# Built forms in a third place, their second part stored first, one raw piece loaded later, and several splits moved

## The chip, the cores and the metric

The kernel runs on one core of a Trainium2 chip. The metric is the device time of one execution in microseconds (us). The times of before are those of three runs; one more execution was profiled, and all rows of the trace come from that one.

## The reference

One input x of 2048 rows and 640 columns is normalized along its rows, without scale or shift. The output is the sum of x and two branches that both read the normalized rows, all in float32:

```python
x = A_x
xn = _layernorm(x, axis=-1)
a = jnp.einsum("bsd,ed->bse", xn, dft_hid_re)
b = jnp.einsum("bsd,ed->bse", xn, dft_hid_im)
y = jnp.einsum("ts,bse->bte", dft_seq_re, a) - jnp.einsum("ts,bse->bte", dft_seq_im, b)
h = jax.nn.gelu(jnp.einsum("bsd,df->bsf", xn, w1) + b1, approximate=True)
return x + y + (jnp.einsum("bsf,fd->bsd", h, w2) + b2)
```

The first branch is a Fourier transform along the hidden dimension (640) and along the sequence (2048), of which the real part is kept; its matrices are inputs. The second is a perceptron with 1536 hidden units.

## The kernel before

**Splits and products.** A float32 operand is split in two: a high part, made by ScalarE (ACT, `high`, line 190), and a low part, made by VectorE (DVE, `low`, line 193) from the operand and its high part. A product of two split operands is three matmuls (`product`, lines 304 to 306): high by high, high by low, low by high. `hidden` (line 326) does the same three by itself. Where the split is of a moving operand, PE can start on the high part and needs the low part one matmul later.

**Order.** The schedule is written out by hand: each engine runs its instructions in the order in which the Python text issues them, and waits only for what an instruction needs. Loads and stores that are issued with `nc.sync` stand in the queue of SP in the same order, those with `nc.gpsimd` in that of POOL.

**Places.** Most of the on-chip memory is a set of named places (`PLACES`, line 144): xab0 to xab3, xc01, xc23, as, r01, rt2. A place holds different things one after the other. When it is opened anew (`place`, `open_place`), the first write into it waits until the last reader of what was there is done. In the perceptron's last block the places hold the split weights: `W1[i]` (the columns of 128 hidden units) and `W2[i]` (their rows of w2). xc23 holds W2[3], W2[4] and W2[5].

**The perceptron.** It runs over four blocks of 512 rows, with twelve chunks of 128 hidden units each. The first block runs chunk by chunk; blocks 1 and 2 share their hidden products in pairs (`pair(k)`, k from 0 to 5, `LASTK` = 5); their hidden units are written to DRAM (`keep`), and `load_unit(i)` brings those of block 2 back as `units[i]` for the outputs of block 2. Around a pair, `beside_pair(k, at)` does work that has nothing to do with it: `prep_w` builds and stores pieces of the hidden transform's weights (`put_w`, line 443 stores them into `wits`), `turn_w` transposes the next raw ones, `put_z` brings the rows of block 3 together for transposing, and `split_unit` splits the hidden units that come next. `split_unit(2 * NF, units[0])` and `split_unit(2 * NF + 1, units[1])` serve the first two outputs of the next loop.

The next loop runs over p from 2 to 9 and does the outputs of block 2; from p = 8 on it also does the first two hidden products of block 3, whose rows have been transposed and split into `xt` by `between(p)`. `between(p)` also loads and splits again what w1 and w2 need (`prep_w1`, `load_w1`, `prep_w2`); w1's raw chunks have three buffers, so the load of one waits for the split of the one three before.

**The loop around the change** (line 1304) does block 3. It runs over i from 0 to 11. A step issues the hidden product of chunk i + 2 (15 matmuls), its gelu and split, the output of chunk i (15 matmuls), `between(2 + NU + i)` for i below 2 (that is p = 10 and 11), and `fourier_step(i)`. Steps 10 and 11 have no hidden product.

**Builds.** `fourier_step(i)` for i from 2 to 9 runs `build(k)` with k = i - 2. A build reads two raw chunks of 128 normalized rows from DRAM (`load_xr`, two steps ahead) and makes from them, by sums and splits, the weights of the transform along the sequence: a first part `xab` (128 partitions of 2 x 1280 numbers, 1280 KB) and a second part `xc` (2 x 896, 896 KB). In the order of the text a build makes most of `xab` first and `xc` last (`part(xc, ...)`, lines 666 and 667, whose ACT half is line 639). The first four builds (h = 1) are for the second half of the transform: their forms are stored to DRAM (`forms_ab`, `forms_c`, lines 1223 and 1224) and loaded again much later. The last four (h = 0) stay in place and are used at once. Builds 0 to 3 and builds 4 to 7 share the places xab0 to xab3. For the second part there are two halves of xc01 and two of xc23; before the change

- builds 0 and 2 use the first half of xc01 and builds 1 and 3 the second half,
- builds 4 and 5 use the two halves of xc01, builds 6 and 7 those of xc23,

so that builds 2, 3, 4 and 5 write where an earlier build was, and wait until that one's store has landed. Build 7's raw rows are loaded by POOL into the second half of xc23 itself, which is opened for that at i = 7 (`load_xr(7)`).

**Raw pieces.** The moving operand of the transform along the sequence comes from `cr` and `ci`, in pieces of four quadrants of 256 KB (`load_a`, line 509). `load_a(0)` and `load_a(1)` load the first two at i = 2. `turn` (line 530) transposes a piece in two halves, `form(n)` splits one half into a slot of `as`, and each entry of the Fourier stage that follows uses one form. `load_a(heir[g])`, issued after a piece's second half is turned, loads the next piece into the same buffer. The pool of raw pieces takes the memory of the raw w1 and w2 (`es_e.close()`), so it waits for their last splits.

**After the loop** ACT takes the five sums of block 3 out of PSUM (line 1383, `ob`), the rest of build 7 and the first entries follow, and from there PE runs through the stages "s" (along the sequence) and "y" (along the hidden dimension) to the end.

Of the kernel before, what the change touches and what calls it, by code (L numbers as in the profile page):

```python
# [15 lines left out]
P = 128  # L16
# [11 lines left out]
def kernel(  # L28
# [78 lines left out]
    NK = 4  # L107
# [385 lines left out]
    def load_a(g):  # L493

        for f in steps_of_load(g):
            f()
# [105 lines left out]
    def load_xr(k):  # L602
        if k >= len(builds):
            return
        h, c = builds[k]
        xr[k] = []
        if k in (0, len(builds) - 1):
            n = 2 if k else 0
            A["xcp", n] = place(f"xc{n}{n + 1}", (P, 2, 2, 7 * P))
        for half in range(2):  # L610
            if k == len(builds) - 1:

                r = A["xcp", 2][:, 1, half, :D].bitcast(F32)
            else:
                r = row_places[:, (2 * k + half) % NC]
            (nc.gpsimd if k == len(builds) - 1 else nc.sync).dma_start(r, xn[half * NS // 2 + h * NK + c])
            xr[k].append(r)

    def build(k, what="abc"):
# [3 lines left out]
            A["sums"] = out_pool.tile([P, 2, 9 * P], F32, tag="zo", bufs=1, name="sums")  # L623
        if k < NK:
            A["xab", c] = place(f"xab{c}", (P, 2, 10 * P))
        A["xc", c] = A["xcp", c // 2 * 2 if h == 0 else 0][:, c % 2]
        ab, xc = A["xab", c], A["xc", c]
        tmp = A["sums"][:, k % 2]

# [398 lines left out]
    def beside_pair(k, at):  # L1028
# [27 lines left out]
        if k == 1:  # L1056
            if at == 2:
                add_sum(0, 2, turn_sum(0, 2, rows, "yt", True))
            if at == 5:
                finish(0, 3, 4)  # L1060
                store_sums(0, 1, 2)
            if at == 3:
                A["wst"] = zo_tile("wst", (P, NB * DQ), F32R)
        if at == {1: 7, LASTK: 4}.get(k, 6):
            turn_w(0, j)
            turn_w(1, j)
# [18 lines left out]
        if k == LASTK - 1 and at in (7, 4):  # L1085
            for c in (12, 13) if at == 7 else (14, 15):
                ln_stats(c)
                scale_by_power(c)
        for n in steps.get(at, ()):
            prep_w(*((j - 1, 3 + n) if n < 0 else (j, n)))  # L1090
        if k == LASTK and at == 2:
# [2 lines left out]
        if k == LASTK and at == 8:  # L1094
            A["gs"] = place("xab1", (P, 5, TB), F32)
            for i in range(3, 8):
                load_unit(i)
            split_unit(2 * NF, units[0])
            for c in range(3 * NC, 4 * NC):
                ln_apply(c)  # L1100
        if k == LASTK and at == 7:
            A["s1"] = place("xab2", (P, ND, TB), F32)
        if k == LASTK and at == 4:
            Z["z"] = place("xab3", (P, NB, DQ), F32)
            put_z(Z["z"], A["rows_3"], nc.gpsimd, nc.sync)
            split_unit(2 * NF + 1, units[1])
            split_unit(2 * NF + 2, units[2])

    units = {}
# [67 lines left out]
    def between(p):  # L1177
# [20 lines left out]
        for n, q in {7: 1, 9: 2, 10: 3}.items():  # L1198
            if p == n:
                open_place(*PLACES[q])  # L1200
        for n in {2: (0,), 3: (1,), 7: (2,), 8: (3,), 9: (4, 5), 10: (6, 7, 8), 11: (9, 10, 11)}.get(p, ()):
            prep_w1(AGAIN[n], 2 * NF + n)
            load_w1(2 * NF + 3 + n)
        if p == 8:
# [1 line left out]
                load_w2(i, nc.gpsimd)  # L1206
        if p == 10:
            open_place(*PLACES[8])
        for n in {10: (9, 10), 11: (11,)}.get(p, ()):
            prep_w2(n)  # L1210
        if p == NU:
            A["s2"] = zo_tile("s2", (P, ND, TB))
            for k, key in ((0, "x"), (2, "us")):
# [3 lines left out]
    def fourier_step(i):  # L1217
        if 2 <= i < 2 + 2 * NK:
            k = i - 2
            build(k, "abc" if i < 9 else "a")  # L1220
            load_xr(k + 2)
            if k < NK:
                nc.sync.dma_start(forms_ab[k], A["xab", k].bitcast(F32))
                nc.sync.dma_start(forms_c[k], A["xc", k].bitcast(F32))
        if i == 9:
            A["r01"] = place("r01", (P, 2, 2, 2, TB), F32)
            turn(0, 0)
# [75 lines left out]
    load_xr(1)  # L1303
    for i in range(NF):
        g = 3 * NF + i
        if i == 2:
            es_e.close()
            A["raw"] = pool("rawp")
            load_a(0)
            load_a(1)  # L1310
        if i >= NF - 2:
            output(g)
        else:
# [1 line left out]
            gelu(g + 2, acc)  # L1315
            output(g)

        if i < 2:
            between(2 + NU + i)
        fourier_step(i)  # L1320


# [672 lines left out]
```

## Time and profile before

| what | value |
|---|---|
| median of 3 runs | 854.04 us |
| lowest and highest run | 853.31 and 854.73 us |
| the profiled execution | 855.07 us |
| its span, first to last instruction | 853.3 us |
| mean clock granted to PE | 0.999 of full speed |
| DMA moved | 171.72 MB, mean 201 GB/s |
| PE busy in 222 to 250 us | 28.00 of 28.00 us |
| ACT busy in 290.3 to 305.5 us | 8.15 of 15.20 us |

The span is what the trace covers; the profiled execution's own time is 1.8 us longer. PE is TensorE's matmuls, PEld its weight loads, DVE VectorE, ACT ScalarE, POOL GpSimd and SP SyncE. In a time line a row gives start and duration, engine, line, operation, the tiles written and read, and their count; in brackets stands how long the engine was idle before, and what released it. A row "A <- B: 3.1, 4, 1.4" of the waits says that A waited for B 3.1 us in total, 4 times, at most 1.4. Matmuls overlap: a matmul is listed with about 0.39 us, while the next one starts some 0.23 us after it.

### The profile page before, as it was taken

What the parts mean: (1) busy time and instruction counts of PE and PEld (TensorE: products, weight loads), DVE (VectorE), ACT (ScalarE), POOL (GpSimd) and SP (SyncE); (2) the same over time, 40 slices, a digit from 0 to 9 for tenths busy, and PEclk for the clock granted to TensorE, in tenths of its full rate; (3) what the DMA queues carried; (4) which work ended last, traced back from release to release, by engine and by line L of the source; (5) the groups of instructions that cost most, each with busy time, mean ns of one, the idle gap of its engine ahead of it and who ended that gap; (6) DMA issues with size and microseconds to landing.
All of it is one profiled execution on the core that took longest, in us unless ns stands there. A gap on an engine that the chain in (4) does not pass through costs nothing.

```text
span 853.3 us, 10719 instructions
## 1 busy us (share of the span) xinstructions
PE 842.1 (99%) x3719; PEld 694.8 (81%) x3719; DVE 695.1 (81%) x920; ACT 373.7 (44%) x546; POOL 90.5 (11%) x166
## 2 busy tenths in 40 slices
PE   9999999999999999999999999999999999999997
PEld 7888888888788867888888888888888888888886
DVE  6978888777666689799888878899688998867995
ACT  6655656645555554334443432323224332344350
POOL 3440023256200000000000000000000000010102
PEclk9999999999999999999999999999999999999999
DMA  7996569779879779586445795637357997175453
GB/s 233 289 263 167 122 172 299 236 236 365 263 217 347 310 141 205 133 186 150 141 112 156 246 280 140 157 101 217 133 166 231 251 245 283 50 276 180 117 149 87
DMA packets 194454, 171.72 MB, mean 201 GB/s; under 512 B 57920, under 2 KB 164928, under 8 KB 193888
## 3 DMA queue, kind: packets, MB, share of 16 engines
q1 hardware_dynamic: 181664, 134.53, 58.9%
q0 software_dynamic: 10560, 35.99, 12.0%
q10 hardware_dynamic: 2176, 0.52, 0.3%
q8 instruction: 29, 0.48, 0.2%
q14 instruction: 25, 0.20, 0.1%
HBM read 119.87 MB, written 47.19 MB: 196 GB/s over the span
## 4 chain that ended last, share of the span: by engine, by line
PE 82%; DMA 8%; DVE 4%; ACT 2%; issue 1%; SPq 1%; POOL 1%; DVEq 0%; POOLq 0%; ACTq 0%
PE banks L305 25%; PE banks L306 25%; PE banks L304 25%; PE banks L326 5%; DMA forms_c<-xc 3%; DMA w1r<-in_B_w_dram 1%; DMA w2r<-in_B_w_dram 1%; DMA raw<-in_A_dft_seq_re_dram 1%; DMA xab<-rt 1%; PE banks L695 1%; SPq L282 1%; DVE rt L530 1%; DMA wit<-wst 0%; ACT xc L639 0%; DVE as L193 0%
## 5 line engine op out<-in xcount | busy, mean ns | idle before, releaser
L190 ACT ACTIVATE as<-r 128x1024 fp32r<-128x1024 f32 x80 | 84.9, 1062 | 170.2 <-PE banks L306 146.5
L305 PE MATMUL banks<-as,xab 128*128 128x512 f32 (+1 forms) x375 | 146.0, 389 | 3.1 <-DVE as L193 3.1
L306 PE MATMUL banks<-as,xab 128*128 128x512 f32 (+1 forms) x375 | 145.5, 388 | 0.0
L304 PE MATMUL banks<-as,xab 128*128 128x512 f32 (+1 forms) x375 | 145.5, 388 | 0.0
L193 DVE TENSOR_TENSOR as<-r,as 128x1024 fp32r<-128x1024 f32 x80 | 97.2, 1216 | 37.9 <-ACT as L190 37.7
L304 PE MATMUL banks<-as,xc 128*128 128x512 f32 x244 | 94.9, 389 | 0.0
L305 PE MATMUL banks<-as,xc 128*128 128x512 f32 x244 | 94.9, 389 | 0.0
L306 PE MATMUL banks<-as,xc 128*128 128x512 f32 x244 | 94.9, 389 | 0.0
L305 PEld LDWEIGHTS banks<-as,xab 128*128 128x128 f32 x375 | 70.4, 188 | 19.1 <-DVE as L193 4.7
L304 PEld LDWEIGHTS banks<-as,xab 128*128 128x128 f32 x375 | 70.4, 188 | 14.6 <-ACT as L190 0.2
L306 PEld LDWEIGHTS banks<-as,xab 128*128 128x128 f32 x375 | 70.4, 188 | 14.4
L190 ACT ACTIVATE as<-rt 128x1024 fp32r<-128x1024 f32 x37 | 39.3, 1063 | 82.4 <-PE banks L306 62.7
L326 PE MATMUL banks<-xt,xab 128*128 128x512 f32 x240 | 57.4, 391 | 0.7 <-DVE xt L193 0.7
L193 DVE TENSOR_TENSOR as<-rt,as 128x1024 fp32r<-128x1024 f32 x37 | 45.0, 1216 | 11.8 <-ACT as L190 11.8
L326 PEld LDWEIGHTS banks<-xt,xab 128*128 128x128 f32 x240 | 44.7, 188 | 11.0 <-DVE xt L193 1.8
L305 PEld LDWEIGHTS banks<-as,xc 128*128 128x128 f32 x244 | 45.8, 188 | 9.5
L306 PEld LDWEIGHTS banks<-as,xc 128*128 128x128 f32 x244 | 45.8, 188 | 9.5
L304 PEld LDWEIGHTS banks<-as,xc 128*128 128x128 f32 x244 | 45.8, 188 | 9.5
L305 PE MATMUL banks<-hs,xc 128*128 128x512 f32 x120 | 46.8, 390 | 0.2 <-DVE hs L193 0.2
L306 PE MATMUL banks<-hs,xc 128*128 128x512 f32 x120 | 46.7, 389 | 0.0
L304 PE MATMUL banks<-hs,xc 128*128 128x512 f32 x120 | 46.7, 389 | 0.0
L1428 POOL DMA_DIRECT2D seed_x<-seeds x1 | 0.5, 546 | 401.4 <-DVE y L469 401.4
(307 smaller groups left out, 1719.9 us busy)
## 6 DMA issues: line engine op xcount, KB each, us to landing
raw<-in_A_dft_seq_re_dram SPq DMA_DIRECT2D x64, 256.0 KB, 5.3
raw<-in_A_dft_seq_im_dram SPq DMA_DIRECT2D x64, 256.0 KB, 5.2
w1r<-in_B_w_dram SPq DMA_DIRECT2D x144, 80.0 KB, 3.4
wit<-wst POOLq DMA_DIRECT2D x15, 384.0 KB, 4.3
wit<-wst POOLq DMA_DIRECT2D x20, 256.0 KB, 4.2
forms_ab<-xab SPq DMA_DIRECT2D x4, 1280.0 KB, 12.6
ws<-wit SPq DMA_DIRECT2D x13, 384.0 KB, 5.2
row<-xn SPq DMA_DIRECT2D x14, 320.0 KB, 8.3
```

The source lines that it names most:

```text
L190: nc.scalar.activation(h, s, AF.Copy)
L193: nc.vector.tensor_tensor(l, s, h.bitcast(F32), op=ALU.subtract)
L282: eng.dma_start(t[q * B : (q + 1) * B], v[q, :, :, f0 : f0 + P])
L304: nc.tensor.matmul(acc, wh, mh, start=first, stop=False, skip_group_check=goes_on)
L305: nc.tensor.matmul(acc, wh, ml, start=False, stop=False, skip_group_check=goes_on)
L306: nc.tensor.matmul(acc, wl, mh, start=False, stop=last, skip_group_check=goes_on)
L326: nc.tensor.matmul(acc, W1[i][:, a, j * P : (j + 1) * P], XT[j][:, b], start=n == 0, stop=n == len(steps) - 1)
L530: nc.vector.transpose(held(pieces[g][2], u).rearrange("p c (n i) -> p c n i", i=B), r.rearrange("p n (c i) -> p c n i", i=B))
L695: nc.tensor.matmul(wacc, warm[:, :P], warm, start=True, stop=True)
L1428: nc.gpsimd.dma_start(A["seed"], seeds[:, c0:c1])
```

## The change

1. **A third place.** The second part of build 3 goes to the second half of xc23, not to that of xc01. xc23 is opened in build 3 (i = 5), not with build 7's rows (i = 7). Builds 4 to 7 use the same places as before.
2. **Stores.** Of each of the first four builds, `forms_c` is stored before `forms_ab`.
3. **Raw pieces.** `load_a(0)` stays at i = 2, but behind the work that `between(12)` now does there; `load_a(1)` is issued at i = 7.
4. **Last splits of w1 and w2.** The six w1 splits that stood at p = 10 and 11, three each, stand at 10, 11 and 12, two each; of the three w2 splits there is one at each.
5. **First two units.** `split_unit` of unit 0 goes ahead of `prep_w` at place 8 of the last pair, and that of unit 1 ahead of `turn_w` at place 4.

```diff
@@ load_xr
-        if k in (0, len(builds) - 1):
-            n = 2 if k else 0
-            A["xcp", n] = place(f"xc{n}{n + 1}", (P, 2, 2, 7 * P))
+        if k == 0:
+            A["xcp", 0] = place("xc01", (P, 2, 2, 7 * P))
@@ build
-        A["xc", c] = A["xcp", c // 2 * 2 if h == 0 else 0][:, c % 2]
+        if k == NK - 1:
+            A["xcp", 2] = place("xc23", (P, 2, 2, 7 * P))
+        A["xc", c] = A["xcp", c // 2 * 2 if k >= NK - 1 else 0][:, c % 2]
@@ beside_pair
+        if k == LASTK and at == 4:
+            split_unit(2 * NF + 1, units[1])
         if at == {1: 7, LASTK: 4}.get(k, 6):
             turn_w(0, j)
             turn_w(1, j)
...
+        if k == LASTK and at == 8:
+            split_unit(2 * NF, units[0])
         for n in steps.get(at, ()):
             prep_w(*((j - 1, 3 + n) if n < 0 else (j, n)))
...
             for i in range(3, 8):
                 load_unit(i)
-            split_unit(2 * NF, units[0])
             for c in range(3 * NC, 4 * NC):
                 ln_apply(c)
...
             put_z(Z["z"], A["rows_3"], nc.gpsimd, nc.sync)
-            split_unit(2 * NF + 1, units[1])
             split_unit(2 * NF + 2, units[2])
@@ between
-        for n in {2: (0,), 3: (1,), 7: (2,), 8: (3,), 9: (4, 5), 10: (6, 7, 8), 11: (9, 10, 11)}.get(p, ()):
+        for n in {2: (0,), 3: (1,), 7: (2,), 8: (3,), 9: (4, 5), 10: (6, 7), 11: (8, 9), 12: (10, 11)}.get(p, ()):
             prep_w1(AGAIN[n], 2 * NF + n)
             load_w1(2 * NF + 3 + n)
...
-        for n in {10: (9, 10), 11: (11,)}.get(p, ()):
-            prep_w2(n)
+        if p in (10, 11, 12):
+            prep_w2(p - 1)
@@ fourier_step
             if k < NK:
+                nc.sync.dma_start(forms_c[k], A["xc", k].bitcast(F32))
                 nc.sync.dma_start(forms_ab[k], A["xab", k].bitcast(F32))
-                nc.sync.dma_start(forms_c[k], A["xc", k].bitcast(F32))
@@ the loop over i
-        if i == 2:
-            es_e.close()
-            A["raw"] = pool("rawp")
-            load_a(0)
-            load_a(1)
...
-        if i < 2:
+        if i < 3:
             between(2 + NU + i)
+        if i == 2:
+            es_e.close()
+            A["raw"] = pool("rawp")
+            load_a(0)
+        if i == 7:
+            load_a(1)
         fourier_step(i)
```

## The prediction

> **What bounds the kernel now.** I read the head of the page first, then the waits of the tensor engine, then a table of stretches, and last the time lines of PE, ACT and DVE around each stop.
>
> ```profile
> span 853.3 us, 10719 instructions
> PE 842.1 (99%) x3719; PEld 694.8 (81%) x3719; DVE 695.1 (81%) x920; ACT 373.7 (44%) x546; POOL 90.5 (11%) x166
> ```
>
> ```profile
> PE banks L305 <- DVE as L193: 3.1, 4, 1.4
> PE banks L326 <- DVE xt L193: 0.7, 2, 0.4
> PE banks L304 <- ACT hs L190: 0.6, 1, 0.6
> PE banks L305 <- DVE hs L193: 0.4, 2, 0.2
> ```
>
> ```profile
> 250.00:290.30 40.30, 40.30 (x180) 33.36 (x179) 28.30 (x66) 22.24 (x47) 1.10 (x2) 1.00 1.01 345
> 290.30:305.50 15.20, 14.38 (x63) 11.29 (x61) 12.60 (x27) 8.15 (x16) 0.00 (x0) 1.00 0.18 72
> 305.50:330.40 24.90, 21.80 (x93) 16.77 (x92) 22.13 (x26) 12.79 (x18) 0.00 (x0) 1.00 1.09 205
> 330.40:848.90 518.50, 518.45 (x2306) 430.01 (x2306) 439.46 (x428) 186.54 (x205) 13.33 (x22) 1.00 0.65 176
> ```
>
> PE is the bound: after 330.4 it is busy 518.45 of 518.50 us, and between 250 and 290.3 all the time. Nothing but its few stops can be won, and almost all of them lie between 290.3 and 330.4 (columns: stretch, its length, then busy us of PE, PEld, DVE, ACT, POOL, the clock, DMA share, GB/s). The time line of PE shows them:
>
> ```profile
> 290.51 3.56 PE L326 MATMUL banks<-xt,as 128*128 128x512 f32 x15
> ...
> 301.46 0.50 PE L304 MATMUL banks<-hs,rt 128*128 128x512 f32 x1 [0.59 <-ACT hs L190]
> 302.19 0.51 PE L305 MATMUL banks<-hs,rt 128*128 128x512 f32 x1 [0.23 <-DVE hs L193]
> ...
> 306.63 0.50 PE L305 MATMUL banks<-as,xab 128*128 128x512 f32 x1 [0.76 <-DVE as L193]
> ...
> 330.35 0.50 PE L305 MATMUL banks<-as,xab 128*128 128x512 f32 x1 [1.41 <-DVE as L193]
> 330.68 0.39 PE L306 MATMUL banks<-as,xab 128*128 128x512 f32 x1
> ```
>
> The 15 matmuls at 290.51 are the last hidden product (step i=9). Fifteen starts take 3.40 us when nothing stops them (the next group begins at 293.91), so 0.2267 each. From 290.51 to 330.68 the program has 152 starts (15 hidden, 45 of three outputs, 90 of five entries of the Fourier stage, and two), which is 34.46 us; it took 40.17. So **5.7 us** are lost here, and that is the ceiling for this part. A step of this loop, one hidden and one output, is 6.80.
>
> The stops begin because the last gelu is late. ACT shows why:
>
> ```profile
> 271.36 1.05 ACT L639 ACTIVATE xc<-sums 128x256 fp32r<-128x256 f32 x2 [4.12 <-DMA forms_c<-xc]
> ...
> 279.63 1.04 ACT L639 ACTIVATE xc<-sums 128x256 fp32r<-128x256 f32 x2 [4.47 <-DMA forms_c<-xc]
> ...
> 286.43 1.04 ACT L639 ACTIVATE xc<-sums 128x256 fp32r<-128x256 f32 x2 [3.00 <-DMA forms_c<-xc]
> ...
> 293.23 1.05 ACT L639 ACTIVATE xc<-sums 128x256 fp32r<-128x256 f32 x2 [3.00 <-DMA forms_c<-xc]
> 294.18 0.67 ACT L346 ACTIVATE ab<-banks,b1c 128x512 f32<-128x512 f32 x1
> ...
> 295.42 1.23 ACT L639 ACTIVATE xab<-row 128x384 fp32r<-128x384 f32 x3
> ...
> 300.07 0.67 ACT L346 ACTIVATE ab<-banks,b1c 128x512 f32<-128x512 f32 x1
> ...
> 307.77 1.06 ACT L190 ACTIVATE as<-r 128x1024 fp32r<-128x1024 f32 x1 [1.33 <-DVE r L530]
> 308.74 2.98 ACT L1383 ACTIVATE ob<-banks,b2c 128x512 f32<-128x512 f32 x5
> ```
>
> Builds 2 to 5 each stop before they write their second part, until the store of the build two before has landed: 14.6 us in four waits. Gelus stand behind them on ACT. The gelu of 300.07 belongs to the product that ended near 293.9, so ACT is 6 us behind PE. DVE takes this over:
>
> ```profile
> 302.98 2.36 DVE L530 STREAM_TRANSPOSE r<-raw 128x1024 f32<-128x1024 f32 x2
> ...
> 312.05 0.43 DVE L469 TENSOR_TENSOR xab<-xc,xab 128x256 fp32r<-128x256 f32 x1 [0.62 <-ACT xab L639]
> ...
> 318.40 1.23 DVE L193 TENSOR_TENSOR as<-r,as 128x1024 fp32r<-128x1024 f32 x1
> ...
> 329.07 1.22 DVE L193 TENSOR_TENSOR as<-rt,as 128x1024 fp32r<-128x1024 f32 x1
> ```
>
> From 302.98 it works almost without a break (22.13 of the 24.90 us after 305.5); the low part that ends at 330.29 releases the matmul of 330.35. Whatever moves this chain earlier moves PE by as much, up to the ceiling.
>
> **The change, part by part. The third place.** Build 3 no longer shares a place with builds 1 and 5. So build 5 waits for the store of build 1 (four steps older), build 4 for that of build 2, and build 6 for none, as before. The writes of build 3 wait instead until PE has read W2[3..5], the end of output(5), which is 293.91 + 3.40 - 4 x 6.80 = 270.1. Build 3 stands behind gelu(7), whose product ends at 293.91 - 4 x 6.80 = 266.7; with the gelu (1.24, from 294.18 to 295.42) and its own first part (at least the 1.23 of 295.42) it reaches that write not before 269.2. So the wait is at most 0.9 us, and what stands behind it on ACT is gelu(8), whose product ends at 273.5: bounds 0 and 0.9, taken as 0. **Stores first.** The second part's store no longer stands behind 1280 KB of the first. On SP the row loads still go ahead of both. The first part's store now leaves only when the whole build is done; its place is rewritten four steps (27 us) later, so I cost this at nothing.
>
> **The raw piece.** SP's time line and the chain in order of time show the stream; the other two rows are the times to landing of the raw pieces between 250 and 330, and of the row loads of L616:
>
> ```profile
> 250.56 7.53 SPq L509 DMA_DIRECT2D raw<-in_A_dft_seq_re_dram  x8
> ```
>
> ```profile
> 256.86 7.94 DMA raw<-in_A_dft_seq_re_dram
> ```
>
> ```profile
> DMA to landing us min/median/max: 3.0/6.7/9.8
> ```
>
> ```profile
> DMA to landing us min/median/max: 3.4/8.1/11.9
> ```
>
> Eight raw pieces go out from 250.56 and the last lands at 264.80. Less the 3.0 that a lone one needs, that is 11.2 for eight, 5.6 for four. Taking load_a(1) out puts rows, stores and builds 5.6 us further ahead in a queue whose DMA share is 1.01 of the window. Against this, load_a(0) now waits for the last two w1 splits behind gelu(4), and a gelu is 1.24 us of ACT, of which I count 1.0. Load_a(1) itself goes out at i=7, behind the rows of build 6 on SP, and lands 5.6 after those (which come at 289.4 to 290.8, below), near 296. Its transposes began near 306.5 before (302.98, two transposes, a form of 1.2), so they would near 301 in the new order. That is 5 us of cover; beyond it, a late piece costs one for one.
>
> What binds ACT then? A build without waits takes 4.65 us (295.42 to 300.07), with its gelu some 6.0 against a step of 6.80, so ACT catches up by 0.8 a step. The rows of build 6 were there by 295.4 (no wait before it), and by the median of 8.1 after their issue near 294. Less 5.6, plus 1.0: 289.4 to 290.8. Build 6 starts there, the last gelu 4.65 later, at 294.1 to 295.5; PE alone would allow 294.3. The shift S of that gelu is thus **4.6 to 5.8 us**. Downstream DVE and ACT work back to back, so S carries on, with one new limit: the five ob evictions of 308.74 read the banks of output(11), which without stops ends near 304.3. If the first has to wait for all of it, S becomes 308.74 - 304.3 = 4.4; bank by bank, it doesn't bind. I take S = 5.2, the middle of 4.6 and 5.8, and keep 4.4 and 5.8 for the range. The matmul of 330.35 can come 5.6 earlier at most, so the gain is S: **5.2 us**. After 330.4 PE has no stop, ACT waits for PE at almost each form, and all moves along.
>
> By the Trainium skill, page "DMA: Bandwidth & Descriptors", section "Issuing engines are not separate DMA queues", transfers from all issuing engines share the same 16 DMA engines; so the rows that POOL loads for the last build take time from SP's stores. The trace agrees: the releases of 271.36 and 279.63, with POOL's row loads between, are 8.27 apart where the next are 6.80 apart. It changes no term, as those loads lay in the stream before too.
>
> **The splits.** This part pays at one place and is lost at another:
>
> ```profile
> 197.34 0.50 PE L305 MATMUL banks<-hs,xc 128*128 128x512 f32 x1 [0.15 <-DVE hs L193]
> ...
> 219.79 0.96 PE L326 MATMUL banks<-xt,xab 128*128 128x512 f32 x3 [0.34 <-DVE xt L193]
> 221.11 1.55 PE L326 MATMUL banks<-xt,xab 128*128 128x512 f32 x5 [0.36 <-DVE xt L193]
> ```
>
> ```profile
> 195.15 1.57 DVE L409 STREAM_TRANSPOSE row<-row 128x640 f32<-128x640 f32 x2
> 196.63 1.25 DVE L193 TENSOR_TENSOR hs<-g,hs 128x512 fp32r<-128x512 f32 x2
> ...
> 215.34 0.71 DVE L263 STREAM_TRANSPOSE ztx<-xab 128x512 f32<-128x512 f32 x1 [2.22 <-DMA wit<-wst]
> ```
>
> ```profile
> 201.78 1.12 ACT L190 ACTIVATE wst<-row 128x256 fp32r<-128x256 f32 x4 [4.15 <-DMA wit<-wst]
> ```
>
> The low part at 196.63 stands behind two transposes of 1.57; ahead of them it makes its matmul of 197.34, and about 0.4 us of PE (0.15 idle, and the gap between matmul starts) goes. But PE stops again at 219 for xt, on a chain of DVE that waits at 215.34 for a store, and through ACT at 201.78 for an earlier one. That chain does not wait for PE, so PE comes 0.4 earlier and waits 0.4 longer: **nothing**. At 201.78 the stop is long enough (4.15) to hide that the wst splits ahead of it leave some 1 us later; with that cover gone it costs up to 1 us at 219. Bounds: +0.4 and -1.0. The w1 splits that move to i=2 are needed by products from 283.7 on (290.51 - 6.80), 30 us away, and PE does not stop from 222 to 290: nothing.
>
> Sum against the profiled run: 855.07 - 5.2 = 849.9 (span 853.3 to 848.1). The median of the three runs lies 1.03 lower, so I give **848.8**.
>
> **Rivals.** *The stream keeps the lag.* A build's rows and stores are 640 + 896 + 1280 = 2816 KB, and 6.80 us between releases makes 424 GB/s: a rate as slow as PE's step, so lost time in the queue is never made up. If POOL's rows (8.27 - 6.80 = 1.5) and a slower start of the raw piece (another 1) fall ahead of build 6, S is 5.2 - 2.5 = 2.7 and the time 851.3. For it: DMA share 1.01. Against: both were in the old stream too. The Trainium skill, "DMA: Bandwidth & Descriptors", section "Specifications", has a fabric ceiling of 435 GB/s; by that rule 424 is full speed, and swapping two stores buys no stream time, which the trace agrees with. *The change doesn't do what it says:* load_a(1), last in the queue, lands 5 us after my 301, near 306; the transposes start where they did, only the 0.6 and 0.2 us stops at 301.46 and 302.19 go, given back at 306.63. About 854.0. For it: it has the whole stream ahead of it; against: 5 us of cover. *Slower:* the raw rows of build 7 go into the half of the third place that build 3 filled, so POOL, which waited for PE alone before, must now wait for build 3's store. That landed at 293.2; less 5.6, plus 1.0, and less 3.1 for the 1280 KB that it no longer stands behind (6.80 x 1280 / 2816), it is 285.5. POOL has nothing queued behind (0.00 busy up to 330.4), but build 7 has: it began 1.24 after the gelu of 300.07. Rows that land later than 301.3 make the new kernel slower, one for one: at 304, 2.7 us, or 856.7. For it: one more thing to wait for, in a full stream; against: it takes 15.8 us to landing, where the longest row load took 11.9.
>
> **How the numbers follow.** Forecast (gain 4.4 to 5.7) 0.62; stream keeps the lag (gain 1.8 to 4.4) 0.21; the change does not do it (within 1.7 us) 0.11; slower 0.06. The range reaches from the ceiling with the split's 0.4 and 0.3 for the spread of runs, 854.04 - 5.7 - 0.4 - 0.3 = 847.6, to a gain of 1.8, 852.2, which holds a good part of the second case. 0.2% is 1.7 us, about what a measurement of this kernel can tell from no change: faster 0.83, same 0.11, slower 0.06.
>
> **What will show it.** Right: no wait of xc (L639) on forms_c of more than 1 us; the last gelu at 294 to 296; PE idle between 290 and 330 below 0.5 us; the stop at 197 gone and that at 219 longer by 0.4; still no stop after. Wrong: row or raw waits in the builds or transposes, a stop of the ob evictions on PE, the last build late for its rows, or a stop at 219 longer than 0.5 beyond the old one.

## The result, and the profile after

| kernel | median, us | lowest to highest | runs |
|---|---|---|---|
| before, beside it | 853.67 | 852.96 to 854.73 | 6 |
| changed | 849.03 | 848.51 to 850.56 | 6 |

The ratio is 0.9949 (95% interval 0.9936 to 0.9962): faster, by 4.6 us in the medians. The profiled execution of the changed kernel took 849.01 us, that of before 855.07, so the two traces differ by more, 6.06. The head of its page, the waits of PE and the stretches (columns as before):

```profile
span 847.2 us, 10714 instructions
PE 840.1 (99%) x3719; PEld 694.7 (82%) x3719; DVE 694.3 (82%) x920; ACT 374.3 (44%) x546; POOL 90.4 (11%) x166
```

```profile
PE banks L696 <- POOL warm L684: 2.0, 1, 2.0
PE banks L326 <- DVE xt L193: 0.7, 2, 0.4
```

```profile
250.00:290.30 40.30, 40.30 (x179) 33.37 (x178) 33.04 (x77) 25.08 (x51) 1.10 (x2) 1.00 0.98 346
290.30:305.50 15.20, 15.20 (x69) 12.59 (x68) 13.68 (x20) 10.21 (x18) 0.00 (x0) 1.00 0.68 145
305.50:330.40 24.90, 24.90 (x112) 20.56 (x111) 22.34 (x25) 10.20 (x14) 0.00 (x0) 1.00 1.14 210
330.40:842.60 512.20, 512.20 (x2281) 424.96 (x2279) 433.19 (x422) 184.51 (x203) 13.33 (x22) 1.00 0.64 176
```

The waits of PE for `as` and `hs` are gone; in this execution the start and the two short stops near 219 remain. PE is busy all the time from 250 to 842.6. The gain is counted in matmuls: the same 40.1 us of each kernel, first before, then after, hold 25 more of them, and 25 x 0.2267 = 5.67.

```profile
290.30:330.40 40.10, 36.18 (x154) 28.07 (x152) 34.74 (x52) 20.94 (x33) 0.00 (x0) 1.00 0.75 155
```

```profile
290.30:330.40 40.10, 40.10 (x179) 33.15 (x178) 36.02 (x45) 20.41 (x30) 0.00 (x0) 1.00 0.97 185
```

The time line of ACT after shows where this comes from:

```profile
270.94 0.42 ACT L640 ACTIVATE xc<-sums 128x256 fp32r<-128x256 f32 x1 [0.44 <-DVE sums L469]
...
280.15 0.69 ACT L346 ACTIVATE ab<-banks,b1c 128x512 f32<-128x512 f32 x1 [0.63 <-PE banks L326]
...
286.95 0.69 ACT L346 ACTIVATE ab<-banks,b1c 128x512 f32<-128x512 f32 x1 [0.80 <-PE banks L326]
...
289.06 0.53 ACT L640 ACTIVATE xab<-row 128x384 fp32r<-128x384 f32 x1 [0.75 <-DMA row<-xn]
290.60 0.83 ACT L640 ACTIVATE xab<-row 128x384 fp32r<-128x384 f32 x2 [1.01 <-DMA row<-xn]
...
293.94 0.67 ACT L346 ACTIVATE ab<-banks,b1c 128x512 f32<-128x512 f32 x1
...
295.18 0.92 ACT L640 ACTIVATE xab<-xc 128x384 fp32r<-128x384 f32 x2
...
302.61 2.98 ACT L1387 ACTIVATE ob<-banks,b2c 128x512 f32<-128x512 f32 x5
```

No second part waits for a store any more; that of build 3 (270.94), in the third place, waits 0.44 for DVE and not for PE. At 280.15 and 286.95 it is ACT that waits for PE. One lag is left: build 6 waits for its two rows, and the last gelu comes at 293.94 instead of 300.07.

PE's trace, matmul by matmul, gives the rest of the 6.06: 0.25 us lie ahead of 197, where the two texts still agree and only the executions differ; 0.4 are won at the stop of 197, of which 0.3 are lost again at 219; then 5.71 between 290 and 330; after that the two run alike (517.88 and 517.90 us to the last matmul).

### The profile page after: what moved, and what is told of

It reads as the page before. It is cut to its first block, busy times and chain, and to the rows that moved or that the text cites. A ratio compares the mean times of both kernels' runs of the same rounds, so it can differ in the third digit from the quotient of the medians.

```text
span 847.2 us, 10714 instructions
## 1 busy us (share of the span) xinstructions
PE 840.1 (99%) x3719; PEld 694.7 (82%) x3719; DVE 694.3 (82%) x920; ACT 374.3 (44%) x546; POOL 90.4 (11%) x166
## 4 chain that ended last, share of the span: by engine, by line
PE 94%; DVE 2%; DMA 1%; POOL 1%; issue 1%; ACT 0%; POOLq 0%; DVEq 0%; ACTq 0%
PE banks L306 28%; PE banks L304 28%; PE banks L305 28%; PE banks L326 9%; DMA wit<-wst 1%; PE banks L696 1%; POOL wit L444 0%; DVE wst L193 0%; DVE ztx L263 0%; PE banks L712 0%; DVE xt L193 0%; POOL late_units L979 0%; POOL mv L1025 0%; DVE st L219 0%; DVE hs L193 0%
## 5 line engine op out<-in xcount | busy, mean ns | idle before, releaser
L305 PEld LDWEIGHTS banks<-as,xab 128*128 128x128 f32 x375 | 70.4, 188 | 14.6
L190 ACT ACTIVATE as<-rt 128x1024 fp32r<-128x1024 f32 x37 | 39.3, 1062 | 82.2 <-PE banks L306 62.7
L326 PEld LDWEIGHTS banks<-xt,xab 128*128 128x128 f32 x240 | 44.7, 188 | 11.4 <-DVE xt L193 2.3
```

What stands on the lines that cost most here:

```text
L190: nc.scalar.activation(h, s, AF.Copy)
L305: nc.tensor.matmul(acc, wh, ml, start=False, stop=False, skip_group_check=goes_on)
L326: nc.tensor.matmul(acc, W1[i][:, a, j * P : (j + 1) * P], XT[j][:, b], start=n == 0, stop=n == len(steps) - 1)
```

## The experiments

The expectations name two theories. By the **queue** theory the last gelu comes when the rows of build 6 have landed, and each part of the change acts through what stands ahead of those rows in the queue of SP. By the **places** theory the waits for `forms_c` made ACT late, and what counts is the third place that takes them away. In the expectations of the first four runs the queue theory is called 'stream'.

The table holds what I read from every profiled execution. *Start*: issue of the first quadrant of `load_a(0)`. *Store*: landing of the last of the eight stores. *Row*: landing of the last row of build 6. *Lag*: start of the last gelu less the end of its product (start of the product plus 3.40). *Lost*: from the start of that product to the 152nd start after it, less 34.46. The medians and ratios are of all runs of each kernel, the ratios against before on the same chip. The four groups of runs had a before of their own (853.67, 854.42, 853.95 and 853.87), so kernels of different groups are compared by their ratios. All other columns are of one execution each.

| kernel | start | store | row | gelu | lag | lost | median | ratio (95%) |
|---|---|---|---|---|---|---|---|---|
| before | 250.6 | 293.1 | 294.7 | 300.07 | 6.16 | 5.72 | 853.67 to 854.42 | 1 |
| after | 251.3 | 287.4 | 290.6 | 293.94 | 0.38 | 0.01 | 849.03 | 0.9949 (0.9936 to 0.9962) |
| a_no_third | 250.5 | 289.6 | 293.5 | 296.81 | 3.46 | 3.02 | 850.49 | 0.9962 (0.9947 to 0.9977) |
| a_ab_first | 249.4 | 285.3 | 288.5 | 292.24 | 0.20 | 0.30 | 849.65 | 0.9950 (0.9932 to 0.9969) |
| a_raw_early | 250.9 | 291.4 | 292.8 | 296.29 | 2.87 | 2.42 | 850.31 | 0.9960 (0.9945 to 0.9975) |
| a_units_back | 251.8 | 289.7 | 292.6 | 295.93 | 2.95 | 2.51 | 850.11 | 0.9946 (0.9928 to 0.9964) |
| b_raw_late | 250.2 | 288.2 | 292.2 | 295.53 | 3.10 | 2.67 | 850.30 | 0.9957 (0.9945 to 0.9970) |
| b_third | 250.0 | 290.3 | 291.8 | 295.73 | 2.54 | 2.09 | 850.98 | 0.9964 (0.9952 to 0.9977) |
| b_c_first | 250.3 | 292.0 | 293.5 | 296.93 | 4.25 | 3.81 | 852.61 | 0.9984 (0.9975 to 0.9993) |
| after_again | 250.0 | 286.8 | 289.7 | 293.03 | 0.47 | 0.02 | 847.99 | 0.9934 (0.9921 to 0.9946) |
| c_ab_tile | 249.3 | 285.3 | 288.2 | 291.98 | 0.20 | 0.00 | 847.88 | 0.9929 (0.9917 to 0.9941) |
| c_ab_units_back | 250.3 | 287.8 | 290.9 | 294.30 | 2.15 | 1.70 | 848.89 | 0.9934 (0.9922 to 0.9946) |
| c_raw0_late | 276.0 | 285.3 | 295.7 | 299.07 | 5.84 | 5.39 | 854.82 | 1.0009 (1.0000 to 1.0018) |
| c_both | 275.1 | 286.1 | 296.1 | 299.50 | 7.59 | 7.13 | 853.59 | 0.9996 (0.9986 to 1.0005) |

Two rules stand in it. Where PE loses more than 1.5 us, the loss is the lag less 0.43 to 0.46, in ten executions; with a lag below 0.5 it is at most 0.3. And the gelu comes 3.36 after the last row in eight of the fourteen. So one time, that of the last gelu, decides this part, as the prediction's S had it.

### One part undone

**a_no_third**: the changed kernel, with build 3's second part back in xc01.

```diff
-        if k == 0:
-            A["xcp", 0] = place("xc01", (P, 2, 2, 7 * P))
+        if k in (0, len(builds) - 1):
+            n = 2 if k else 0
+            A["xcp", n] = place(f"xc{n}{n + 1}", (P, 2, 2, 7 * P))
...
-        if k == NK - 1:
-            A["xcp", 2] = place("xc23", (P, 2, 2, 7 * P))
-        A["xc", c] = A["xcp", c // 2 * 2 if k >= NK - 1 else 0][:, c % 2]
+        A["xc", c] = A["xcp", c // 2 * 2 if h == 0 else 0][:, c % 2]
```

> The changed kernel, but build 3 writes its second part into the half of xc01 where build 1 was, as before the change. Theory 'places' (the third place is what takes the store waits away): builds 3 and 5 wait for stores again, two of the four old waits come back at 3 us or more each, the last gelu is 3 us or more late, and the time is 852 or more. Theory 'stream' (the raw piece's 5 us in the queue and the stores' order are what count): in the changed kernel's trace the store of build 1 landed at 269.7 and build 3 writes at 270.9, so it does not wait; that of build 3 landed at 284.2 and build 5 writes at 283.4, a wait of 0.8; POOL loads build 7's rows some 14 us earlier, so they push 1.5 us of stream ahead of builds 4 and 5, waits of about 1 each. The last gelu is at most 1 us late and the time 849.0 to 850.2.

Measured 850.49. The waits for `forms_c` came back with 3.8 us, not 14.6, and the longest was 2.0. What costs more is another effect: POOL, which again waits for PE alone, issues the rows of build 7 at 270.02, in the middle of the stream, and those of build 6 land at 291.3 and 293.5. They are issued at 278.45, as early as in the changed kernel (278.81), so the waits for places did not hold them up; they are in flight for longer. The time is between the two expectations, 0.3 above that of the 'stream' theory, by which the last gelu was to be at most 1 us late; it is 2.9 later than in the changed kernel's trace.

**a_ab_first**: the first part stored first again.

```diff
-                nc.sync.dma_start(forms_c[k], A["xc", k].bitcast(F32))
                 nc.sync.dma_start(forms_ab[k], A["xab", k].bitcast(F32))
+                nc.sync.dma_start(forms_c[k], A["xc", k].bitcast(F32))
```

> The changed kernel with forms_ab stored before forms_c again. Each second part lands 3.1 us later (1280 KB at the stream's rate). Theory 'stream': build 2 waits 1.0 (266.0 against 265.0 in the changed kernel's trace), build 4 2.8 (279.6 against 276.8), and the rows that POOL loads for build 7 land 3.1 later, at 296.6 and 298.0, when build 7 starts at 295.2; so the chain behind it starts 1.5 to 2.9 late and 851.0 to 852.0 is measured. Theory 'places': with a third place the order of the two stores is free, 849.0.

Measured 849.65, which the interval does not part from the changed kernel's. The 'stream' expectation, 851.0 to 852.0, is missed. ACT waited 4.5 us for two stores, but made it up: at 285.44 it waited for PE again. The rows of build 7 were to come too late, and landed at 293.9 and 294.6, about when build 7 began (293.91). The last row of build 6 landed 39.1 us after the start of the stream, that of the changed kernel 39.3. With the other two parts in, the order of the stores is worth nothing that these four runs show.

**a_raw_early**: `load_a(1)` back at i = 2.

```diff
             load_a(0)
-        if i == 7:
             load_a(1)
```

> The changed kernel with the second raw piece loaded at i = 2 again, right behind the first. Theory 'stream': everything behind it in the queue comes 5.2 to 5.6 us later; build 6's rows land at 295.8 to 296.2, its end and the last gelu 4.65 later near 300, and almost the whole gain goes: 853.0 to 854.0. Theory 'places': no store wait longer than 1 us comes back, the last gelu is at 296 or earlier, and most of the gain stays: 849.0 to 850.5.

Measured 850.31. The time lies in the range of the 'places' theory. The last gelu comes at 296.29, between the two expectations and nearer to that of the places: from the start of the stream the row needs 42.0 us, where it needs 39.3 and 39.7 in the two traces of the changed kernel, so the piece costs some 2.5 us at the rows by these traces, not 5.6. Two stops of PE return, on its time line:

```profile
320.73 0.50 PE L305 MATMUL banks<-as,xab 128*128 128x512 f32 x1 [0.37 <-DVE as L193]
...
326.56 0.50 PE L305 MATMUL banks<-as,xab 128*128 128x512 f32 x1 [1.45 <-DVE as L193]
```

**a_units_back**: the first two units split where they were (part 5 undone).

```diff
-        if k == LASTK and at == 4:
-            split_unit(2 * NF + 1, units[1])
...
-        if k == LASTK and at == 8:
-            split_unit(2 * NF, units[0])
...
+            split_unit(2 * NF, units[0])
...
+            split_unit(2 * NF + 1, units[1])
```

> The changed kernel with the splits of the first two units where they were. By the prediction this is worth nothing: the stop of PE at 197 comes back (0.4), the stop for xt near 219 is 0.35 shorter, and the time stays at 849.0 within 0.2 by the time line of PE. The rival, that the earlier splits are worth what they take off at 197: 849.4 and the stop at 219 unchanged.

Measured 850.11, the ratio that of the changed kernel. The stop at 197 came back, and PE reached the product at 290 0.6 us *earlier* than in the changed kernel's trace, since the stop at 219 was 1.1 shorter, where 0.35 was expected. The rows landed 2.0 later, though nothing of the stream differs. Both are more than the splits can account for, and I read them as the spread between executions.

### One part alone

Three kernels are the kernel before with one part of the change each, beside the changed kernel again.

**b_raw_late**: `load_a(1)` at i = 7 only.

```diff
             load_a(0)
+        if i == 7:
             load_a(1)
```

> The kernel before with one edit: the second raw piece is loaded at i = 7. Old places, old store order. Theory 'queue' (what counts is what stands ahead of build 6's rows and of the stores in SP's queue): 5.2 us leave the queue ahead of all of them; the store that build 5 waits for lands at 288 instead of 293.1, build 6 starts at 290.4 and the last gelu is at 295, so this edit alone brings 4 to 5 us, about 0.9945 of the time before. Theory 'places': waits for stores remain at builds 3, 4 and 5, the last gelu stays at 298 or later, and it brings 2 us or less, 0.9977 or more.

**b_third**: only part 1 of the change.

```diff
-        if k in (0, len(builds) - 1):
-            n = 2 if k else 0
-            A["xcp", n] = place(f"xc{n}{n + 1}", (P, 2, 2, 7 * P))
+        if k == 0:
+            A["xcp", 0] = place("xc01", (P, 2, 2, 7 * P))
...
-        A["xc", c] = A["xcp", c // 2 * 2 if h == 0 else 0][:, c % 2]
+        if k == NK - 1:
+            A["xcp", 2] = place("xc23", (P, 2, 2, 7 * P))
+        A["xc", c] = A["xcp", c // 2 * 2 if k >= NK - 1 else 0][:, c % 2]
```

> The kernel before with one edit: build 3's second part goes to the second half of xc23. Theory 'queue': build 5's wait for the last store goes, but build 4 still waits for that of build 2 (285), and build 6's rows land near 293 (the 1.5 us that POOL's rows took ahead of them move behind); the last gelu is near 298, 2 us earlier. POOL's rows now wait for the last store (291.6) and land near 300, at or after the start of build 7. It brings 1 to 2 us, 0.9977 to 0.9988. Theory 'places': the store waits were the cause, and this alone brings 4 us or more, 0.9953 or less.

**b_c_first**: only the order of the stores.

```diff
-                nc.sync.dma_start(forms_ab[k], A["xab", k].bitcast(F32))
                 nc.sync.dma_start(forms_c[k], A["xc", k].bitcast(F32))
+                nc.sync.dma_start(forms_ab[k], A["xab", k].bitcast(F32))
```

> The kernel before with one edit: forms_c stored before forms_ab. Theory 'queue': each of the four stores that are waited for lands 3.1 us earlier, that of build 5 at 290 instead of 293.1, but build 6's rows still land at 294.7, as nothing left the queue; the last gelu comes 1 to 2 us earlier (298 to 299). It brings 1 to 2 us, 0.9977 to 0.9988. A rival: since ACT is behind from the first store wait on, 3.1 us less at each wait carry over whole and it brings 3 us, 0.9965.

**after_again**: the changed kernel once more.

> The changed kernel once more, beside the three kernels with one edit each. Both theories: 0.9945 to 0.9955 of the time before. Theory 'queue' also says that its last gelu moves from execution to execution with the landing of build 6's rows: about 3.4 us after the second of them, wherever that falls between 289 and 293.

The gains in the medians are 3.65, 2.97 and 1.34 us; together they would be 7.96, and the changed kernel beside them gains 5.96. They overlap, because PE can win no more than the 5.7 us that it lost.

By their expectations, the raw piece alone (0.9957, last gelu at 295.53) comes near what the queue theory gave, about 0.9945 and 295, and far from that of the places. The third place alone (0.9964) lies between the two, better than the queue theory gave (0.9977 to 0.9988). The order of the stores alone (0.9984) brings what the queue theory gave, though its gelu, at 296.93, is earlier than the 298 to 299 expected; the rival of 3 us (0.9965) lies outside its interval. The changed kernel itself came out slightly better (0.9934) than the 0.9945 to 0.9955 expected, its gelu 3.36 after the last row.

What each does to the stream is read from the table as *row* less *start*: 44.2 before, 42.0 with the raw piece later, 41.8 with the third place, 43.2 with the stores swapped, 39.7 with all. The raw piece alone has an odd split. Its last store lands 38.0 after the start instead of 42.6, so 4.6 are won, not far from the 5.6 of the prediction. But then the last row needs 4.0 us after that store, where it needed 1.6. The stretches between the two, first in before, then in b_raw_late, show why:

```profile
293.10:294.70 1.60, 1.60 (x9) 1.33 (x8) 0.82 (x2) 1.47 (x3) 0.00 (x0) 1.00 0.15 56
```

```profile
288.20:292.20 4.00, 4.00 (x20) 3.30 (x19) 2.75 (x5) 2.77 (x6) 0.00 (x0) 1.00 1.20 183
```

In before little else is under way any more (DMA share 0.15). In b_raw_late the share is 1.20, at 183 GB/s: the raw piece, issued 1.5 us behind the rows, moves beside them, as SP's time line there has it:

```profile
278.79 1.32 SPq L616 DMA_DIRECT2D row<-xn  x2
280.27 6.43 SPq L509 DMA_DIRECT2D raw<-in_A_dft_seq_re_dram  x4
```

Every kernel with `load_a(1)` at i = 7 and `load_a(0)` at i = 2 has 2.9 to 4.0 us between last store and last row, every one with both at i = 2 has 1.4 to 1.6. By this measure, half of what the move of the raw piece wins for the stores is given back at the rows.

The third place alone takes 2.2 us out of the way to the last store. It also leaves ACT waiting:

```profile
ACT xc L640 <- DMA forms_c<-xc: 8.0, 2, 4.1
```

That row of its waits shows two of 8.0 us together, in place of four of 14.6. POOL's rows, for which the prediction had read 1.5 us, moved behind the rows of build 6 (issued at 290.88) as in the changed kernel; POOL's time line of before and of after:

```profile
270.57 1.10 POOL L616 DMA_DIRECT2D xc<-xn  x2 [36.29 <-PE banks L306]
```

```profile
284.79 1.10 POOL L615 DMA_DIRECT2D xc<-xn  x2 [50.86 <-DMA forms_c<-xc]
```

Before, these 640 KB ran at 270 to 279, ahead of the rows of build 6. Now POOL waits for build 3's store, and they run behind them. By the Trainium skill, page "DMA: Bandwidth & Descriptors", section "Issuing engines are not separate DMA queues", loads of another engine take their share of the same 16 DMA engines. The runs agree: with these rows ahead again, a_no_third had its last row 43.0 us after the start, against 39.3 and 39.7.

The late rows have another possible cause. Build 6's rows take the buffers of build 4's, so SP issues them only when build 4 has read its own, and in before that is 7 us later than in after:

```profile
285.85 0.82 SPq L616 DMA_DIRECT2D row<-xn  x2
```

```profile
278.81 1.52 SPq L615 DMA_DIRECT2D row<-xn  x2
```

But in before the DMA engines still had the stores to move: their share was 1.02 from 279.6 to 286.4, at 421 GB/s where the prediction had worked out 424, and 0.95 from there to 293.2. The second row was in flight for 8.5 us there and for 11.4 in after, so it landed 4.2 us later, not 7. With the engines full until 293, 1.6 us ahead of that landing, an earlier issue alone would have had little to win; this is argued from these shares, and no run tried it.

### The stop at 219, and the start of the stream

**c_ab_tile**: the changed kernel, with the last tile of `put_w` in the buffers "ab" instead of "zt". The transposes of block 3 (`ztx`) use "zt" too, and the second of them no longer has to wait until that tile has been stored.

```diff
-                t = mr.tile([P, 2, 2 * P], F32R, tag="zt", bufs=2, name=name)
+                t = mr.tile([P, 2, 2 * P], F32R, tag="zt" if j < ND - 1 else "ab", bufs=2, name=name)
```

> The changed kernel, with the last hidden weight of window 4 built in a buffer of the gelus (tag ab) instead of one that the transposes of block 3 need (tag zt). If the stop of PE near 219 comes from the wait of the second transpose for the store out of that buffer (2.2 us in the kernel before), that wait goes, the chain of xt is 2 us earlier, and both stops near 219 (1.3 to 1.7 us in all) go. Of that, what the last gelu and the form chain behind it can't follow (they hang on the rows of build 6, and the fifth entry has 0.24 us to spare in the changed kernel) comes back near 324. Net 0.2 to 1.7 us less than the changed kernel, 0.992 to 0.9945 of the time before. Rival: the stop near 219 comes from the ping-pong of ACT and DVE over five transposes, and it stays: no change.

**c_ab_units_back**: the same, with part 5 undone as in a_units_back.

> The same, and the splits of the first two units where they were before the change. If the earlier splits were worth nothing only because PE waits for xt at 219 anyway, then with that wait gone their 0.4 us at 197 must stay: PE reaches 224 about 0.4 later than in the kernel with the other buffer alone. If not, PE reaches 224 at the same time in both.

The wait of DVE for that store (2.24 us in the changed kernel's trace) is gone in c_ab_tile, and so are both stops near 219; the waits of PE have one row left:

```profile
PE banks L696 <- POOL warm L684: 2.0, 1, 2.0
```

Its ratio, 0.9929, is the lowest here and lies in the range expected, but its interval overlaps those of the changed kernel: that the edit wins time is not shown. With the stop at 219 gone, the split is seen alone: in c_ab_units_back PE's time line has the old gap,

```profile
196.49 0.39 PE L304 MATMUL banks<-hs,xc 128*128 128x512 f32 x1
197.02 0.50 PE L305 MATMUL banks<-hs,xc 128*128 128x512 f32 x1
197.36 0.40 PE L306 MATMUL banks<-hs,xc 128*128 128x512 f32 x1
```

0.87 for what two starts take in 0.45, and its product at 290 comes 0.37 later than in c_ab_tile (288.75 and 288.38). So the 0.4 of part 5 is real where PE has no stop behind it.

Whether it is eaten at 219 depends on the execution. Twenty matmul starts there, from 216 on, take 4.53 us in c_ab_tile and c_ab_units_back. They took 5.95 in before and 6.30 in the changed kernel's first trace, but 5.00 in its second (after_again), and 4.57 in b_raw_late, which is the kernel before up to there. The store that DVE waits for released it at 215.3, 214.9, 214.0 and 213.8 in these four. So the stop of 219 is between nothing and 1.8 us, more than part 5 can bring.

The stop at 219 may have a second price. `load_a(0)` waits for the last splits of w1, these for raw chunks that are loaded after earlier splits, and all of that comes later when PE stops. ACT's wait for the chunk ahead of gelu(4), in after and in c_ab_tile:

```profile
246.47 0.74 ACT L190 ACTIVATE as<-w1r 128x640 fp32r<-128x640 f32 x1 [4.50 <-DMA w1r<-in_B_w_dram]
```

```profile
244.36 0.74 ACT L190 ACTIVATE as<-w1r 128x640 fp32r<-128x640 f32 x1 [4.10 <-DMA w1r<-in_B_w_dram]
```

The stream starts at 251.3 in the one and 249.3 in the other. But it starts at 250.0 in after_again, with a stop, and at 250.3 in c_ab_units_back, without one, so the two traces alone don't show that the stop is the cause. That an earlier load of these chunks would start the stream sooner is argued, and was not tried.

### The other piece later too

**c_raw0_late**: the changed kernel with `load_a(0)` at i = 6; **c_both** adds the edit of c_ab_tile.

```diff
         if i == 2:
             es_e.close()
             A["raw"] = pool("rawp")
+        if i == 6:
             load_a(0)
```

> The changed kernel with the first raw piece loaded at i = 6, so that it leaves the queue ahead of builds 2 to 6 too. Theory 'queue': rows and stores land 5 us earlier, builds no longer wait for rows (1.8 us in front of build 6 in the changed kernel), the last gelu comes when its product ends and the scatter between executions shrinks; but PE has no stop left there, so the time is that of the changed kernel within 0.5 us, 0.9935 to 0.995. Against: the raw piece lands near 291, 5 us ahead of its transpose; if it is late, PE stops near 304 and the time is longer.

> Both of these edits. If the stop near 219 goes with the buffer and the builds have time to spare without the first raw piece, nothing is given back at 324: 1.3 to 1.7 us less than the changed kernel, 0.992 to 0.9935 of the time before, and the narrowest scatter of all.

Both lose the whole gain (854.82 and 853.59), against their expectations, which had left out what the issue of the piece costs SP. Their twelve runs each also spread more widely (852.52 to 857.02 and 852.25 to 856.09) than the 23 of before beside them (852.90 to 855.70), where a smaller scatter was expected. SP's and ACT's time lines of c_raw0_late:

```profile
275.96 7.82 SPq L509 DMA_DIRECT2D raw<-in_A_dft_seq_re_dram  x4
283.89 2.04 SPq L615 DMA_DIRECT2D row<-xn  x2
```

```profile
294.18 0.52 ACT L640 ACTIVATE xab<-row 128x384 fp32r<-128x384 f32 x1 [6.18 <-DMA row<-xn]
295.74 0.83 ACT L640 ACTIVATE xab<-row 128x384 fp32r<-128x384 f32 x2 [1.04 <-DMA row<-xn]
...
299.07 0.67 ACT L346 ACTIVATE ab<-banks,b1c 128x512 f32<-128x512 f32 x1
```

The builds run on time, and the last store lands at 285.3, as early as anywhere. But the issue of the raw piece holds SP for 7.8 us, and the rows of build 6, next in its order, go out at 283.89 instead of 278.81. They come at 295.7, and ACT waits 7.2 us for them. There are no waits for a place here, and yet the time is that of before. So being free of those waits is not enough to make this kernel fast: what stands ahead of the last rows makes it slow even without them.

## Why the prediction was right, and which of its terms were not

The 848.8 us and its range hold: 849.03, and 847.99 beside the single parts. The stretch is the one it named, and nothing followed after 330.

**What bounds it: right.** The ceiling of 5.7 was real, and the changed kernel reaches it (5.71 in the trace, against the 5.2 taken). S counted against PE is 6.16 - 0.38 = 5.78, the upper end of 4.6 to 5.8. The rows of build 6 land at 289.0 and 290.6 (289.4 to 290.8 predicted), the last gelu comes at 293.94 (294.1 to 295.5). One thing that was named as a sign of being wrong did come, ACT's waits for the two rows of build 6 (0.75 and 1.01 us), and they cost PE nothing. The limit of 4.4 by the `ob` evictions doesn't bind: they begin at 302.61, and no stop of PE follows.

**The gain by the medians is smaller than that of the traces** (4.6 and 6.0 in two comparisons, against 6.06). The trace of before is of an execution that is 1.4 above the median beside it, and PE reached 290.51 there, where the kernels with one part alone, the same up to 250, came at 289.0 to 289.8: the twenty starts at 219 took 4.57 to 5.14 us in those three and 5.95 in before. Nor has each execution of the changed kernel its rows at 290.6: its runs reach from 847.9 to 850.6, and in a_units_back and c_ab_units_back lags of 2.95 and 2.15 are seen where the stream's text is the same.

**The sum was right, two of its terms were not.** *The raw piece* was to bring the rows 5.6 earlier. It brings the stores 4.6 earlier, but the rows only 2.2 (44.2 to 42.0), because the piece that was moved behind them then shares the DMA engines with them. *POOL's rows* were said to change no term, "as those loads lay in the stream before too". They don't lie there any more: with the third place they move behind the rows of build 6. The trace had 1.5 us for them, and the prediction used this only for the rival, as something that falls ahead of build 6. Third place and stores, taken for nothing in the stream, brought 2.4 and 1.0 when alone, each read from one execution, and the 1.0 is less than executions differ by. Thus 5.6 - 1.0 = 4.6 was predicted for the rows, and 4.2 (after) and 5.1 (after_again) came, by other shares. The raw piece was taken too large and the two other parts too small, and that the errors cancel is luck. The 1.0 for a later start was 0.8 in after; in after_again the stream started 0.6 earlier than in before.

**The remaining 2.0 of S** (row to gelu, 5.35 before, 3.36 after) is ACT's: it no longer comes to build 6 late from a wait of build 5. But this needs no third place. In b_raw_late, where build 5 still waits for the store of build 3, that wait ends at 288.26, ahead of the rows (290.5 and 292.2), and the gelu comes 3.37 after the last of them; with the stores swapped alone it is 3.44. The rest is the row against PE, 294.7 - 290.5 before and 290.6 - 290.15 after: 3.8 of the 5.8, most of it.

**The splits: right that they bring nothing, the mechanism only in part.** From PE's time line, before and after, ahead of and behind the stop:

```profile
196.80 0.39 PE L304 MATMUL banks<-hs,xc 128*128 128x512 f32 x1
197.34 0.50 PE L305 MATMUL banks<-hs,xc 128*128 128x512 f32 x1 [0.15 <-DVE hs L193]
197.68 0.40 PE L306 MATMUL banks<-hs,xc 128*128 128x512 f32 x1
```

```profile
196.55 0.39 PE L304 MATMUL banks<-hs,xc 128*128 128x512 f32 x1
196.77 0.39 PE L305 MATMUL banks<-hs,xc 128*128 128x512 f32 x1
197.00 0.39 PE L306 MATMUL banks<-hs,xc 128*128 128x512 f32 x1
```

The lead grows from 0.25 to 0.68 and is 0.36 at 290. In the prediction the chain of DVE behind the store stands still. It did not; its step of 215.34 came 0.41 earlier:

```profile
214.93 0.71 DVE L263 STREAM_TRANSPOSE ztx<-xab 128x512 f32<-128x512 f32 x1 [2.24 <-DMA wit<-wst]
```

PE came earlier by 0.74 at 216 and waited 0.35 longer. In after_again the stop was shorter than in before, not longer. What holds is that PE waits there for that chain: c_ab_units_back shows that the 0.4 stays when the wait for the store is cut. The w1 and w2 splits, which were costed at nothing, show no stop of PE anywhere between 222 and 290.

**The rivals.** *The stream keeps the lag* did not come; its two dangers, POOL's rows and the start (0.8 later in after), were one gain and one loss. *The change doesn't do it* failed with the raw piece, which lands at 294.5 to 296.4 ("near 296") with the transposes near 300.4. *Slower* came close to biting, if not to deciding: POOL issues at 284.79 (285.5 predicted), the rows of build 7 land at 293.5 and 294.9, and build 7 begins at 295.18, only 0.3 us later. The point from which the kernel would be slower than before, 301.3, was 6 us off.

**Open:** what moves the start of the stream, its speed and the stop at 219 between executions, and whether the order of the stores is worth anything beside the other two parts. The third place does two things, it takes waits away and moves POOL's rows, and no run has one without the other. Part 4 was undone in no run; that it costs nothing is read from PE's time line, and what it does to the start of the stream is not shown.

## What to carry to other kernels

Find the one landing on which the last late instruction hangs, and list all that stands ahead of it in every queue; in this kernel a load moved "later" helped only when it went behind that landing, and even there it took a share of the engines when it was issued right behind. Parts that shorten the same wait overlap, and together they win no more than the bound engine lost, so price a combination by the lag that is left, not by the sum of its parts. A waiting engine's loads are part of a place's price or gain: a place that frees one engine can hold up another, here to the good.

## What the runs showed of the hardware

- The issue of a transfer is no fixed cost. Four raw quadrants took SP 1.99 us at 251.33 in the changed kernel, with nothing else in the stream (DMA share 0.00 in the 1 us ahead), and 7.82 in c_raw0_late at a share of 1.02 (424 GB/s); the third of the four alone took 6.06. What is next in SP's order waits for as long.
- Executions of kernels whose stream is written alike differ by up to 2 us in the landing of a row at the end of a 40 us stream (38.9 to 40.8 from its start in five of them; 39.3 and 39.7 in the two of the same text), with the granted clock at 0.999 or 1.0 in all.
- A stop of PE costs more than its idle time: in before, the matmul behind the one that had waited (197.34) started 0.34 later, at 197.68, instead of 0.23. With the 0.3 between its own start and its due time, 0.15 of listed idle time made 0.42.
